# Block-sparse attention and a low-rank mixer: pair 5's turn, the first loads and the first scores rearranged

## The chip, the cores and the metric

The kernel runs on one core of one Trainium2 chip. The metric is the device time of one execution in microseconds (us), as the median of several runs. The engines are TensorE (PE, with its weight loads PEld), VectorE (DVE), ScalarE (ACT), GpSimd (POOL) and SyncE (SP, which here only issues transfers). PSUM is the memory that PE writes its products to, in 8 banks; SBUF is the working memory.

## The reference

Block-sparse attention over 4 batches, 8 heads, 768 positions and 64 channels, then a mixer over the result:

```python
scores = (q @ k.T) / sqrt(64)
# a 32x32 block is kept if it is on or next to the diagonal, in the first or last
# block row or column, or sampled; others get -1e9
attn = softmax(scores); x = attn @ v            # [4, 768, 512] with the heads side by side
h = x.transpose(0, 2, 1) @ U @ V                # U: 768x32, V: 32x768, over positions
u = x + h.transpose(0, 2, 1)
out = u + relu(u @ w_ch1) @ w_ch2               # 512 -> 2048 -> 512
```

Inputs and output are float32; the kernel computes its products in float16 with sums in float32.

## The kernel before, in words

Two heads make a **pair** (128 channels); there are 16 pairs, numbers 0 to 3 for batch 0, 4 to 7 for batch 1, and so on. The work of PE, DVE, ACT and SP is put in order by hand: `PLAN` is a long string of words, and each word issues one step. A capital letter is a step of PE, with the PSUM bank as its digit; a small letter takes what an earlier step left for ACT or DVE. Each engine works through its own instructions in the order in which the words name them and waits at semaphores.

- `S` and `B` are scores of batch 0 for one or two chunks of 128 keys (L697, L716). `e` is the exponential on ACT (L706, L724, and L750 for later batches).
- `A` multiplies exponentials with values for batch 0 (L400), `V` does so for later batches. `v` divides by the row sums on DVE (L472 to L477).
- `Q` and `H` are scores of batches 1 to 3 (L741), two heads side by side or one alone. `p` multiplies the exponentials with the mask on DVE (L756).
- `R` turns a loaded pair on PE (six 128x128 transposes against the identity `id16`, L670); `t` copies the result out of PSUM on DVE (L686 for batch 0, L684 for plain pairs). `Z` and `z` do the same for the second head of pair 0 (L337, L344).
- `K` and `k` make the 0/1 mask for the later batches (L656, L662). `M`, `m`, `X`, `Y`, `y`, `D`, `d`, `E`, `g` are the low-rank mixer.
- `U`, `P`, `C` are the first layer (L587), `a` and `b` its relu on ACT or DVE (L599, L601); `W`, `L` are the second layer (L611, L636), `f`, `l` the last sum and the store.

For batch 0 the mask is added inside the score product: `qres` holds the query's 64 channels and 24 one-hot rows, `kres` the key's 64 channels and 24 rows of biases. There are two such sets, `qres[0]`, `kres[0]` and `qres[1]`, `kres[1]`. The biases are computed at the very start from the sampled blocks (DVE, L289 to L296), multiplied with the one-hot rows on PE (`mask_half`, L271) and copied to `kres[0]` by `mask_row` (L279). The first products of `mask_half` lie in bank 6 and in bank 2. The second set's bias rows are copied by DMA (`second_set`).

**The head.** `first_load` fetches queries and keys of pair 0, one head at a time. `first_cast` makes them float16 (L210), `first_turn` turns them on PE in halves of 384 positions (L224), `first_row` copies them out (L282). Eight large dummy matmuls (`keep_warm`, L264) stand ahead of that, two small ones in the middle.

**Loads.** `load_qk(i)` and `load_v(i)` issue the loads of pair i on SP and its casts to float16 on POOL (L137 for whole tiles, L140 for pieces). `loads(i)` issues the loads of pair i+2; each kind has two load buffers. `front(i)` turns a pair by two DMA transposes on SP (L373). Pairs 1 to 4 are turned on PE by `R`, pairs 5 to 15 by `front`. POOL also issues the loads of the weights w1 (`load_w1`, behind the cast of pair 3's keys) and w2 (`hold`, L778 and L357: four one-element copies that wait for pair 5's keys as turned by `front(5)`, then four loads of 512 KB). `begin(i)` runs at the first score of pair i and issues loads at pairs 0, 1, 3 and 4.

Of the kernel before, what the change touches and what calls it, by code (L numbers as in the profile page):

```python
# [19 lines left out]
P = 128  # L20
# [3 lines left out]
def kernel(  # L24
# [43 lines left out]
    small_np = np.zeros((P, NB + 1 + P // 2), np.float32)  # L68
    small_np[:NB, :NB] = (ms_np - 1.0) * -MASK_BIAS
    small_np[:NB, NB] = ii  # L70
    small_np[:, NB + 1 :] = np.eye(P, dtype=np.float16).view(np.float32)

    small_dr = nc.inline_tensor(small_np, name="small_const")
    ohT_dr = nc.inline_tensor(ohT_np, name="one_hot_const")
# [36 lines left out]
    small = consts.tile([P, NB + 1 + P // 2], FP32)  # L111
    ms = small[0:NB, 0:NB]
    iota = small[0:NB, NB : NB + 1]
    id16 = small[:, NB + 1 :].bitcast(FP16)
# [54 lines left out]
    def first_load(h, n, queue):  # L169

        src, nm = ((q, "qld"), (k, "kld"))[n]
        if h == 0:
            lds[nm] = ldpool.tile([P, 2, T, D], FP32, tag="ld" + nm, name=nm)
            sts[0, nm] = stpool.tile([P, T, 2, D], FP16, tag="st" + nm, name="st" + nm)
        if h == 1:
            nc.gpsimd.memset(lds[nm][0:1, h, 0, 0:1], 0.0)
        queue.dma_start(
            out=lds[nm][:, h], in_=src[0, h].rearrange("(p t) d -> p t d", t=T)
        )

# [10 lines left out]
    def second_set():  # L191
        for h in range(2):
            one_hot(1, h)
# [14 lines left out]
    def first_cast(h, n, copy):  # L208
        nm = ("qld", "kld")[n]
        copy(out=sts[0, nm][:, :, h], in_=lds[nm][:, h])  # L210
# [3 lines left out]
    def first_turn(n, c):  # L214

        if n == 1:
            pt = psm([P, HS], FP32)
        elif c == 0:
            pt = pw[:, 1, 0:HS]
        else:  # L220
            pt = psc2()[:, 0, 0:HS]
        first_out[n, c] = pt
        for j in range(3):
            nc.tensor.matmul(  # L224
                pt[0:D, j * P : (j + 1) * P],
                sts[0, ("qld", "kld")[n]][:, 3 * c + j, 0],
                id16,
                start=(j == 0), stop=(j == 2), skip_group_check=True,
            )

    with tc.manual_schedule(
# [13 lines left out]
        first_load(0, 0, nc.sync)  # L245
        nc.scalar.dma_start(out=small, in_=small_dr.ap())
        first_load(0, 1, nc.scalar)
        for h in (1, 0):
            nc.vector.memset(qres[0][(slice(D, P), slice(0, D))[h], h, :], 0.0)
            one_hot(0, h)  # L250
        nc.vector.memset(bias, 0.0)
# [26 lines left out]
        def mask_row(h, c, copy):  # L278
            copy(out=kres[0][mrows[h], h, c * HS : (c + 1) * HS], in_=pks[c][mrows[h]])  # L279

        def first_row(n, c, copy):
            copy(  # L282
                out=(qres, kres)[n][0][drows[0], 0, c * HS : (c + 1) * HS],
                in_=first_out[n, c][0:D],
            )

        neq = consts.tile([P, NB, 3], FP32)
# [14 lines left out]
        for n in range(2):  # L302
            first_cast(0, n, nc.vector.tensor_copy)
        for c in range(2):
            first_turn(0, c)
            first_row(0, c, nc.scalar.copy)
        mask_half(0)
        mask_row(0, 0, nc.vector.tensor_copy)
        first_turn(1, 0)
        first_row(1, 0, nc.scalar.copy)  # L310
        first_turn(1, 1)
        mask_half(1)
        keep_warm(2, 256)
        first_row(1, 1, nc.vector.tensor_copy)
        mask_row(0, 1, nc.vector.tensor_copy)
        mask_row(1, 0, nc.vector.tensor_copy)
        mask_row(1, 1, nc.vector.tensor_copy)
# [3 lines left out]
        nc.vector.memset(Ut, 0.0)  # L321
        load_v(0)
        load_qk(1)
        second_set()
        load_v(1)
        load_mix()


# [105 lines left out]
    S0 S3 e e S5 B0 e Z7 e S3 z Z6 e z B0 A7 A e R6 S3 t A R5 e A B0 t A K6 e A S3 k v A5 A e K6  # L434
    k B0 A A e K7 A K6 k S3 k A K7 e v B0 k S3 e M6 e A5 A m R7 A t B0 K6 R3 e k A A t S6 A e v
    S0 D2 S3 e d A7 A e A S0 K6 A e S3 k K2 A e S5 k A e v S3 R2 e S5 t S0 e M7 e S3 m D2 e B5 d
    A0 D1 e A A d A S3 D2 A e d K1 S5 k R7 e S3 t A S1 e v A5 A e A S3 S6 e K2 A e A k A S3 v B0
    e K7 M6 e k S3 m X5 K7 e A6 Y k A B0 y X7 Y e S3 y E5 A e A g A R7 S0 t A e v S4 S2 e A7 A e
    R1 E6 A t A g A A Q v e e M6 X7 m Y P6 y p H U7 e p H b C e p H b U7 e p H b U6 e p E1 a g p
    V7 Q v e e V6 U7 v p U0 a P1 b C p P6 a C E7 Q a g U6 e e U7 b P6 b p U0 C a U7 p a Q b X6 Y  # L440
    e e P7 y C P6 b C p U0 b a p V7 Q v e e V6 W7 v p U0 W a p Q U6 e e W b U6 p W b p Q f W6 e
    e W p U2 U0 a p a V7 Q v W e e p V7 U2 v W a p Q f W7 e e W p U6 W a p Q U6 e e W b U6 p f a
    p V0 U1 v a V7 U6 v Q a M6 e e W7 m W p D6 U0 d U1 p a D2 D3 a U6 d d D0 U5 a d D6 U1 a d W
    a W Q f D6 W7 e e d W p D0 D6 W d d p W Q f W6 e e W p W W p Q f e e V7 U6 v p a V0 U2 v p
    U7 a U6 a Q b U7 e e U6 b U7 b p U2 a U6 p a U7 a Q b U6 e e U7 b U6 b p U2 a p a V7 Q v e e
    V6 U7 v p U0 b U1 a W6 p a Q W e e W p W U7 f p Q a U6 e e W7 b W p U1 p a V6 Q v W e e p V6
    U2 v W a p Q f W6 e e W p U7 W b p Q U7 e e W b U7 p f U2 a p a V0 v V7 W6 v Q M7 e e W m U7
    p D0 U1 a d U2 p a D7 D3 a U0 d d U1 a D5 D0 a U2 d d U7 a W a W Q f D7 W6 e e d W p D1 D7 W
# [452 lines left out]
```

## Time and profile before

| | us |
|---|---|
| median of 7 runs (lowest, highest) | 284.62 (283.57, 287.79) |
| the profiled execution | 283.55 |
| its span, from first to last instruction | 281.7 |
| first score on PE | 6.74 |
| first exponential on ACT | 7.27 |
| first exponential of pair 1 on ACT | 16.81 |
| first score of batch 1 on PE | 43.64 |
| first product of the first layer | 45.64 |
| busy time of PE, DVE, ACT, POOL | 273.7, 194.0, 177.9, 75.5 |

The span is the profiled one; the profiled execution is 1.85 us longer than its span, and 1.07 us shorter than the median. Matmuls on PE overlap one another, so the duration of one (218 ns for a 128-column transpose) is longer than the distance between the starts of two (about 55 ns), and the latter is what a further one costs. In the lines of the timeline the first number is the start in us, the second the busy time, then engine, line, operation, output<-input, shapes and count; square brackets hold the idle time before and what ended it.

### The profile page before, as it was taken

Reading aid. Unit: us, or ns where it says so; the run is one execution under the profiler, and the core shown is the slowest. Engines: PE = TensorE matmul, PEld = TensorE weight load, DVE = VectorE, ACT = ScalarE, POOL = GpSimd, SP = SyncE. Lnnn points to the kernel's source line nnn. Section 1 sums busy time; section 2 is a strip of 40 time slices with the busy share of each in tenths; the row PEclk is TensorE's granted clock in tenths of the full one; section 3 lists DMA queues with packets and bytes.
Section 4 is the critical chain, followed back from the end, with each engine's and each line's share of the span. In section 5 each row is a group of like instructions: output and inputs, shape, how many; then the busy total and the mean of one; then the engine's idle time right before and its main releaser. Section 6 shows DMA issues by size and latency. Waiting matters only on the chain.

```text
span 281.7 us, 6704 instructions
## 1 busy us (share of the span) xinstructions
PE 273.7 (97%) x2768; PEld 159.8 (57%) x2768; DVE 194.0 (69%) x347; ACT 177.9 (63%) x206; POOL 75.5 (27%) x164
## 2 busy tenths in 40 slices
PE   7899999999999999999999999999999999999993
PEld 3577775656464654656455654656547645555552
DVE  5689988988776898778677888776677871003411
ACT  3989998888668656686867555797776303451100
POOL 5369115901577050074352050060000000000000
PEclk9999999999999999999999999999999999999999
DMA  5789997999865654646350843740001062002021
GB/s 166 233 281 298 200 247 184 184 119 268 191 167 204 179 167 105 168 126 195 85 181 37 250 107 95 200 115 9 37 37 40 15 135 77 0 0 77 0 93 57
DMA packets 49118, 37.53 MB, mean 133 GB/s; under 512 B 30464, under 2 KB 45600, under 8 KB 49088
## 3 DMA queue, kind: packets, MB, share of 16 engines
q1 hardware_dynamic: 45968, 32.61, 41.7%
q0 software_dynamic: 2688, 4.19, 10.4%
q8 instruction: 21, 0.34, 0.5%
q10 hardware_dynamic: 432, 0.31, 0.4%
q14 instruction: 9, 0.07, 0.1%
HBM read 27.67 MB, written 6.29 MB: 121 GB/s over the span
## 4 chain that ended last, share of the span: by engine, by line
PE 90%; DMA 3%; DVE 2%; POOL 1%; ACT 1%; SPq 1%; issue 0%; DVEq 0%; ACTq 0%; POOLq 0%
PE ps L587 30%; PE ps L611 29%; PE ps L400 12%; PE ps L741 10%; DMA kld<-in_k_dram 2%; PE ps L697 2%; PE ps L529 2%; PE ps L716 2%; ACT est L724 1%; DMA out_dram<-of 1%; PE ps L670 1%; PE ps L636 1%; PE ps L656 1%; PE ps L566 0%; PE ps L498 0%; DVE xh L477 0%
## 5 line engine op out<-in xcount | busy, mean ns | idle before, releaser
L750 ACT ACTIVATE est<-ps 128x1536 f16<-128x1536 f32 x72 | 100.3, 1449 | 38.7 <-PE ps L741 38.7
L587 PE MATMUL ps<-uT,w1t 128*128 128x384 f16 x512 | 94.3, 326 | 0.0
L611 PE MATMUL ps<-w2t,tT 128*128 128x512 f16 x368 | 87.1, 379 | 0.0
L756 DVE TENSOR_TENSOR est<-est,mask 128x1536 f16<-128x1536 f16 x72 | 69.4, 969 | 15.0 <-ACT est L750 14.9
L599 ACT ACTIVATE tT<-ps 128x384 f16<-128x384 f32 x90 | 43.0, 494 | 43.5 <-PE ps L587 42.3
L587 PEld LDWEIGHTS <-w1t 128*128 128x128 f16 x512 | 47.6, 98 | 36.4 <-issue 5.8
L611 PEld LDWEIGHTS <-tT 128*128 128x128 f16 x368 | 34.5, 98 | 39.6 <-issue 3.8
L400 PEld LDWEIGHTS <-est 128*128 128x128 f16 x1152 | 40.8, 97 | 6.9 <-issue 1.9
L400 PE MATMUL ps<-vt,est 128*128 128x65 f16 x1152 | 43.4, 193 | 0.0
L140 POOL CAST stqld<-qld 128x192 f16<-128x192 f32 x40 | 18.8, 512 | 83.2 <-DMA qld<-in_q_dram 58.4
L619 DVE TENSOR_TENSOR of<-xf,ps 128x512 f32<-128x512 f32 x23 | 15.7, 684 | 27.7 <-PE ps L611 25.7
L601 DVE TENSOR_SCALAR tT<-ps 128x384 f16<-128x384 f32 x38 | 21.1, 555 | 19.0 <-PE ps L587 18.3
L741 PE MATMUL ps<-qpl,kpl 64*128 64x512 f16 (+1 forms) x288 | 31.3, 325 | 0.0
L706 ACT ACTIVATE est<-ps 128x768 f16<-128x768 f32 x30 | 22.5, 813 | 0.6 <-PE ps L697 0.6
L741 PEld LDWEIGHTS <-kpl 64*128 64x128 f16 x288 | 11.7, 94 | 15.9 <-issue 10.4
L477 DVE TENSOR_TENSOR xh<-ps,rcp 128x384 f16<-128x384 f32 x32 | 17.8, 558 | 1.1
L477 DVE TENSOR_TENSOR xf<-ps,rcp 128x384 f32<-128x384 f32 x32 | 17.5, 548 | 0.0
L140 POOL CAST stkld<-kld 128x192 f16<-128x192 f32 x40 | 16.7, 456 | 3.0 <-DMA kld<-in_k_dram 2.6
L541 DVE TENSOR_TENSOR xh<-xh,ps 128x384 f16<-128x384 f16 x28 | 15.4, 549 | 1.7 <-PE ps L529 1.6
L140 POOL CAST vt<-vld 128x192 f16<-128x192 f32 x40 | 15.8, 434 | 0.2 <-DMA vld<-in_v_dram 0.2
L542 DVE TENSOR_TENSOR xf<-xf,ps 128x384 f32<-128x384 f32 x28 | 15.3, 547 | 0.0
L697 PE MATMUL ps<-qres,kres 128*128 128x384 f16 x60 | 14.0, 324 | 0.8 <-DVE kres L279 0.5
(83 smaller groups left out, 149.4 us busy)
## 6 DMA issues: line engine op xcount, KB each, us to landing
vld<-in_v_dram SPq DMA_DIRECT2D x16, 384.0 KB, 5.3
out_dram<-of SPq DMA_DIRECT2D x23, 256.0 KB, 2.1
qld<-in_q_dram SPq DMA_DIRECT2D x15, 384.0 KB, 6.4
kld<-in_k_dram SPq DMA_DIRECT2D x15, 384.0 KB, 4.6
w1t<-in_moe_w_ch_dram POOLq DMA_DIRECT2D x4, 512.0 KB, 8.5
w2t<-in_moe_w_ch_dram POOLq DMA_DIRECT2D x4, 512.0 KB, 9.8
qld<-in_q_dram SPq DMA_DIRECT2D x2, 192.0 KB
uT<-xh SPq DMA_TRANSPOSE x14, 2.8
```

What stands on the lines that cost most here:

```text
L140: last = nc.gpsimd.tensor_copy(out=dst[:, h, ts], in_=ld[:, h, ts])
L400: nc.tensor.matmul(pav[:, sc, :], est[:, n, sc * P : (sc + 1) * P], vts[b % 2][:, 2 * hp + h, g, 0 : D + 1], start=(g == 0 and sc == 0), s ...
L477: nc.vector.tensor_tensor(out=dst, in0=pav[:, :, 0:D], in1=rcp[:, :, None].broadcast_to([P, T, D]), op=ALU.mult,)
L587: nc.tensor.matmul(pt, w1t[:, cc, jj * P : (jj + 1) * P], bts[b].uT[cc][:, c * HS : (c + 1) * HS], start=(cc == 0), stop=(cc == NCC - 1), ...
L599: nc.scalar.activation(out=dst, in_=pt, func=AF.Relu)
L601: nc.vector.tensor_scalar_max(out=dst, in0=pt, scalar1=0.0)
L611: nc.tensor.matmul(po, tts[b, c, jj][:, s * P : (s + 1) * P], w2t[:, jj, :], start=(jj == 0), stop=(jj == NJJ - 1),)
L697: nc.tensor.matmul(ps[:, c], kT[:, h, g * P : (g + 1) * P], qT[:, h, c * HS : (c + 1) * HS], start=True, stop=True,)
L706: lambda: nc.scalar.activation(out=dst, in_=ps, func=AF.Exp, scale=0.125),
L741: nc.tensor.matmul(units[h][:, u * S + lo : u * S + hi], kT[drows[h], g * P : (g + 1) * P], qT[drows[h], lo:hi], start=True, stop=True, sk ...
L750: nc.scalar.activation(out=both[h], in_=units[h].rearrange("p (g n) -> p g n", g=2), func=AF.Exp, scale=0.125,)
L756: lambda: nc.vector.tensor_mul(out=both[h], in0=both[h], in1=mask[:, 2 * j : 2 * j + 2, :]),
```

## The change

1. **First loads.** The queries of pair 0's first head go first on ACT's DMA queue. The small constants move to SP and lose the identity, which becomes a transfer of its own (`eye_dr`, 32 KB) on ACT's queue. The keys of that head come in two halves of 384 positions on SP, the second half behind the one-hot rows.
2. **First casts and turns.** ACT casts the queries and the first key half; DVE casts the second half later. The turns become PE transposes with float16 results. Of the first key half only the first 128 columns (keys and mask rows) are copied ahead of the first score, the rest behind. The two small dummy matmuls go. The second key half (`second_keys`: turn, copy, both copies of the second head's mask rows, and the zeros in `Ut`) comes behind the second score, with `second_set`, `load_v(1)`, `load_mix` and `loads(0)`.
3. **Pair 5** is turned on PE (two more `R` steps and two more `t` copies), not by DMA. The loads of pair 6 are issued behind the copy of pair 5's turned keys. `hold` goes: w2 is loaded behind the cast of pair 5's keys.
4. **PLAN** is another order of the same steps, with 10 `B` and 28 `S` for 9 and 30, and with 83 `a` and 45 `b` for 90 and 38.

```diff
-    id16 = small[:, NB + 1 :].bitcast(FP16)
+    id16 = consts.tile([P, P], FP16)
...
+    halves = (slice(0, T // 2), slice(T // 2, T))
...
-            nc.tensor.matmul(
-                pt[0:D, j * P : (j + 1) * P],
-                sts[0, ("qld", "kld")[n]][:, 3 * c + j, 0],
-                id16,
-                start=(j == 0), stop=(j == 2), skip_group_check=True,
+            nc.tensor.transpose(
+                out=pt[0:D, j * P : (j + 1) * P],
+                in_=sts[0, ("qld", "kld")[n]][:, 3 * c + j, 0],
+                identity=id16,
             )
...
-        first_load(0, 0, nc.sync)
-        nc.scalar.dma_start(out=small, in_=small_dr.ap())
-        first_load(0, 1, nc.scalar)
+        first_load(0, 0, nc.scalar)
+        nc.sync.dma_start(out=small[0:NB], in_=small_dr.ap())
+        first_load(0, 1, nc.sync, halves[0])
+        nc.scalar.dma_start(out=id16, in_=eye_dr.ap())
         for h in (1, 0):
             nc.vector.memset(qres[0][(slice(D, P), slice(0, D))[h], h, :], 0.0)
             one_hot(0, h)
+        first_load(0, 1, nc.sync, halves[1])
...
+        first_cast(0, 0, nc.scalar.copy)
...
         keep_warm(8)
-        for n in range(2):
-            first_cast(0, n, nc.vector.tensor_copy)
+        first_cast(0, 1, nc.scalar.copy, halves[0])
         for c in range(2):
             first_turn(0, c)
-            first_row(0, c, nc.scalar.copy)
-        mask_half(0)
-        mask_row(0, 0, nc.vector.tensor_copy)
         first_turn(1, 0)
-        first_row(1, 0, nc.scalar.copy)
-        first_turn(1, 1)
-        mask_half(1)
-        keep_warm(2, 256)
-        first_row(1, 1, nc.vector.tensor_copy)
+        for c in range(2):
+            mask_half(c)
+        first_row(0, 0, nc.scalar.copy)
+        first_row(0, 1, nc.vector.tensor_copy)
+        mask_row(0, 0, nc.vector.tensor_copy, 0, P)
+        first_row(1, 0, nc.scalar.copy, 0, P)
+        first_row(1, 0, nc.vector.tensor_copy, P)
+        mask_row(0, 0, nc.vector.tensor_copy, P)
+        first_cast(0, 1, nc.vector.tensor_copy, halves[1])
         mask_row(0, 1, nc.vector.tensor_copy)
-        mask_row(1, 0, nc.vector.tensor_copy)
-        mask_row(1, 1, nc.vector.tensor_copy)
...
-        nc.vector.memset(Ut, 0.0)
         load_v(0)
         load_qk(1)
-        second_set()
-        load_v(1)
-        load_mix()
-
+        for h in range(2):
+            one_hot(1, h)
+
+
+    def second_keys():
+        first_turn(1, 1)
+        first_row(1, 1, nc.vector.tensor_copy)
+        for c in range(2):
+            mask_row(1, c, nc.vector.tensor_copy)
+        nc.vector.memset(Ut, 0.0)
...
-    S0 S3 e e S5 B0 e Z7 e S3 z Z6 e z B0 A7 A e R6 S3 t A R5 e A B0 t A K6 e A S3 k v A5 A e K6
+    S0 S3 e e S5 B0 e Z7 e z Z6 S3 z e A7 B0 A A e R6 S3 t A A e A B0 v R6 e S4 t K3 K7 e k k B0
...
-                return nc.vector.tensor_copy(out=dst, in_=pt)
+                nc.vector.tensor_copy(out=dst, in_=pt)
+                if i == HP + 1 and n == 1:
+                    loads(HP)
+                return
...
+            elif i == 3:
+                with tc.issue_after(last.ins):
+                    load_w2(range(0, NJJ, 4))
-
-    def hold(behind):
-
-        for j in range(0, NJJ, 4):
-            nc.gpsimd.tensor_copy(out=w2t[0:1, j, 0:1], in_=behind[0:1, 0:1])
-        load_w2(range(0, NJJ, 4))
...
-        if i == HP:
-            front(HP + 1)
-        elif i == HP + 2:
+        if i == HP + 2:
...
-        for m in {0: (0,), 1: (1, 2), 3: (3,), 4: (4,)}.get(i, ()):
+        for m in {1: (1, 2), 3: (3,)}.get(i, ()):
             loads(m)
-        if i == HP:
-            hold(kpl[1])
...
-        "R": ((turn_qk, i, n) for i, n in each(range(1, HP + 1), (0, 1))),
+        "R": ((turn_qk, i, n) for i, n in each(range(1, HP + 2), (0, 1))),
...
-        for word in PLAN.split():
+        for x, word in enumerate(PLAN.split()):
+            if x == 2:
+                second_keys()
+                second_set()
+                load_v(1)
+                load_mix()
+                loads(0)
```

Around pair 5's two turns the new order reads `S1 g A Y e R6 y A A t A Q v R6 e e t M7 X6 m Y p E7 H`; the old one, without them, `S4 S2 e A7 A e R1 E6 A t A g A A Q v e e M6 X7 m Y P6 y p H` (`R1` there is pair 4's key turn).

## The prediction

> **What bounds the kernel now.** I read the page first (shares of the engines), then the stretches of time, then the timeline of the first 17 us, then the chain of waits around the end of the first batch, then the groups of VectorE (DVE) there.
>
> ```profile
> PE 273.7 (97%) x2768; PEld 159.8 (57%) x2768; DVE 194.0 (69%) x347; ACT 177.9 (63%) x206; POOL 75.5 (27%) x164
> ```
>
> TensorE (PE) is busy for 97% of the span. Where the other 3% lie, the stretches tell (span, busy time of PE, weight loads, DVE, ScalarE, GpSimd, granted clock, DMA share, GB/s):
>
> ```profile
> 6.74:12.00 5.26, 4.02 (x43) 2.64 (x42) 3.35 (x7) 4.47 (x6) 2.25 (x4) 1.00 0.69 229
> 12.00:16.00 4.00, 3.78 (x64) 2.87 (x60) 3.29 (x7) 3.49 (x4) 1.95 (x3) 1.00 0.78 202
> 16.00:46.00 30.00, 29.42 (x422) 21.58 (x421) 26.64 (x61) 27.73 (x33) 13.51 (x17) 1.00 1.01 246
> 46.00:270.00 224.00, 224.00 (x2169) 126.54 (x2169) 155.25 (x259) 139.52 (x161) 54.55 (x128) 1.00 0.48 117
> ```
>
> From 46 us on PE has no gap at all, at full clock. So nothing that the change does to transfers, GpSimd or relus after 46 us can gain time there; it can only lose some. PE's idle time after its first score (6.74 us) is 1.24 + 0.22 + 0.58 = 2.04 us, all before 46 us, and there ScalarE (27.73 of 30) and DVE (26.64 of 30) are nearly full as well. What can be gained is the 6.74 us ahead of the first score and these 2.04 us.
>
> ```profile
> 4.65 0.36 DVE L210 CAST stqld<-qld 128x384 f16<-128x384 f32 x1 [1.12 <-DMA qld<-in_q_dram]
> 5.07 0.52 PE L224 MATMUL ps<-small,stqld 128*64 128x128 f16 x6 [0.71 <-DVE stqld L210]
> 6.74 0.99 PE L697 MATMUL ps<-qres,kres 128*128 128x384 f16 x5
> 7.06 1.60 DVE L279 CAST kres<-ps 24x384 f16<-24x384 f32 x3
> 7.27 2.22 ACT L706 ACTIVATE est<-ps 128x768 f16<-128x768 f32 x3 [0.59 <-PE ps L697]
> 8.24 0.32 PE L697 MATMUL ps<-qres,kres 128*128 128x384 f16 x1 [0.52 <-DVE kres L279]
> 11.09 0.83 POOL L137 CAST stqld<-qld 128x768 f16<-128x768 f32 x1 [1.76 <-DMA qld<-in_q_dram]
> 11.97 0.51 PE L670 MATMUL ps<-small,stqld 128*128 128x128 f16 x6
> 16.81 1.45 ACT L724 ACTIVATE est<-ps 128x1536 f16<-128x1536 f32 x1 [0.20 <-PE ps L716]
> ```
>
> The reader is to see three gates in a row: the first query load (cast at 4.65), the third score, which waits for DVE's mask rows to leave PSUM bank 6 (8.24), and pair 1's query turn, which follows GpSimd's cast, which follows a load (11.92). The last line is pair 1's first exponential.
>
> **Part 1, the head.** Queries go first on ScalarE's queue: issued at 0.75 instead of 1.25. The constants, issued at 0.75, landed in 1.9 us with 44.5 KB; the 192 KB of keys took 3.7 us beside the queries. So the queries land between 2.65 and 4.1; I take 3.2, nearer the lone one. ScalarE's table load and first activation end at 3.15, its cast (0.36 as DVE's to 0.50 as GpSimd's) by 3.7. The key half lands between 3.6 and 4.6 (issued third on SP, at 1.65); its cast takes 0.2 to 0.3. The eight warming matmuls stand from 0.79 to 4.36 with the last one's drain, so PE is free at 4.2 and turns from 4.2 to 5.1 wherever the loads land in those ranges. Nine 128-column turns at 0.055 us between starts and two mask products follow: 4.2 + 0.5 + 0.33 = 5.03. Copies: the first rows left PSUM 0.39 us after the turn's start (5.07 to 5.46) and took 0.47; then a third of the key columns (0.2), beside a third of the mask columns. First score 4.2 + 0.39 + 0.47 + 0.2 + 0.1 = 5.4, at the late end 6.3. **That is 1.3 us earlier (0.4 to 1.4).** The two 256-column warming matmuls that go (0.24 us) stood in PE's wait for the copies and save nothing.
>
> What is late next: the third score writes bank 6, from which DVE still copies the second head's mask rows. DVE's queue from 4.8: query half 0.3, mask 0.2, keys 0.25, mask 0.4, key cast 0.2, mask 0.53, key half 0.3, mask 0.53 (16-bit copies by the 768 columns in 0.56 of L344, 32-bit ones by 1.60/3), with waits for PE 0.3: 7.8 against 8.24. Lead 0.45.
>
> Then pair 1. Its loads stand on SP behind the same things as before; the later ones wait for GpSimd's memset at 3.23 in both. The cast that ends at 11.92 stays, so the turn at 11.97 stays: lead 0 at this point. The new order puts the next double score ahead of the key turn, and the score after it needs the keys' first copy only: by DVE, query copies 12.55 to 13.65, division 14.85 (rows of 1.1 and 1.2), key copy 15.4. Pair 1 starts at 15.5 against 15.96: lead 0.46. Seven mask copies (0.55 each) stand ahead of pair 1's second head on DVE; the second use of bank 6 waits for them until about 19.05, and PE then has 1.6 us of work up to the double score that began at 20.72: 20.6. **Lead 0.15 from here on**; bounds 0 and 1.3.
>
> **Part 2, pair 5's turns.** Two steps R more, 12 matmuls. Two DMA transposes go from SP; the four small copies ahead of the W2 loads on GpSimd go.
>
> ```profile
> 40.27 0.34 PE ps L670 x6
> 43.97 0.57 DVE xh L477
> 44.59 0.51 PE ps L498 x6
> 45.12 0.30 DVE a L502
> 45.47 0.34 PE ps L513
> ```
>
> The row: six turns cost 0.34 us of PE, so +0.67. The query turn stands where PE waits for the last exponential of the batch: hidden, or 0.34 where that wait is gone. The key turn falls between the double score (43.64 + 0.76 = 44.40) and L498 at 44.59, so 0.19 of its 0.34 is hidden. But both copies go to DVE:
>
> ```profile
> L684 DVE COPY qpl<-ps 128x768 f16<-128x768 f16 x1 | 0.6, 559 | 0.3 <-PE ps L670 0.3
> L684 DVE COPY kpl<-ps 128x768 f16<-128x768 f16 x1 | 0.6, 558 | 0.4 <-PE ps L670 0.4
> ```
>
> 0.56 us each. The key copy stands ahead of the copy of `a` (45.12), for which PE's L513 waits: the division ends at 45.0, key copy 45.56, `a` 45.85, L513 at 45.9 instead of 45.47. L529 (0.17) now comes behind that, so the next score starts at 46.23 instead of 46.06, and 0.16 more of PE work is left behind it (0.33 of a first-layer step moved back, 0.17 moved ahead). **Sum +0.33, plus 0.07 for the query turn: +0.4**; bounds +0.15 and 0.67 + 1.12 = +1.8 (nothing hidden on PE or DVE).
>
> The Trainium skill ("TensorE: Matmul & The Clock Gate", Part 4: PE-mode transpose) speaks against this part: a 128x128 turn there is about 275 ns in a kernel, the clock does not come up for it, and a copy has to follow. By that page, as an estimate, the twelve would cost 3.3 us and the total would be near 287.5. The rows of this case show 218 ns from start to end, pipelined to 55 ns between starts, at a granted clock of 1.00; I go by them.
>
> **Part 3, transfers.** Pair 5's loads stand on SP right behind pair 0's `uT` transpose, which moves from 29.9 us to about 24; before, they were issued at 35.31, behind both. Its casts wait for pair 3's turns (27.0 and 32.0 before), so they end near 33 instead of 43. W2 is then issued near 33 instead of 48.38, and its first product stands at 68.5. Its 2 MB and pair 5's 1.15 MB share the DMA engines with w1, whose four loads landed by 38.6 (the landings in the trace); 1.15 MB at the 298 GB/s of the page's fullest slice is 3.9 us: 42.5, and the first product with w1 stands at 45.6. Cover 3.1 us; beyond it each us costs one. Pair 6's loads come behind pair 5's key copy, at 45.6 against 45.54. Cost 0.
>
> Seven relus pass from ScalarE (0.49) to DVE (0.55); 46 to 270 us shows DVE at 155 of 224, cost 0, and 0.4 if all seven land on full stretches. One double score replaces two single ones on ScalarE: 1.35 against 2 x 0.71, 0.07 less.
>
> **Sum.** The profiled execution took 283.55 us, a span of 281.70 and 1.85 around it. 283.55 - 0.15 + 0.4 = 283.8. The median of seven runs lies 1.07 above that execution, so 284.9. A measurement of this kernel tells a change from none at about 1%, 2.85 us.
>
> **Rivals.** *The lead lasts.* If pair 1's queries land early (GpSimd waited 1.76 us for them) nothing holds the order up: -1.3 + 0.4 = -0.9, 284.0; with PE's 2.04 us of waits gone as well -2.9, 281.7, just over 1%. For it: PE, ScalarE and DVE all follow the first score. Against: 11.92 is set by a load whose place does not change, and DVE has little room.
>
> *DVE becomes the bound, slower.* Place: 16 to 46 us, DVE 26.64 of 30. The two copies (1.12) and PE's 0.67 land in full and the lead is eaten: +1.8, 286.4. It decides once DVE's idle time there, 3.4 us now, falls under some 1.1 us. Against: most of that idle time must go first.
>
> *Pair 6 or w1 late, slower.* Pair 6's first score stands at 66.5; before, its transposes were issued by 57.3 and landed 2.8 us later. Cover some 6 to 9 us, against W2's 2 MB in the way. If it were 4 us late beyond that: 288.9.
>
> *The change does not do what it says*, W2 staying behind the w1 loads in GpSimd's queue: no time, as above.
>
> **How the numbers follow.** No change as computed 0.60; the lead lasts 0.23, a quarter of that beyond 1%; DVE 0.11; late transfers 0.06. Faster by over 1% 0.07, slower by over 1% 0.08 (late transfers, and 0.02 of DVE's case), within 1% 0.85. The likeliest case alone spans 283.8 to 286.0 (its lead 0 to 1.3, its cost 0.15 to 0.8, and half a us of scatter in the median); the range takes in most of the first two rivals: 282.6 to 287.0.
>
> **What would show it.** Right: first score near 5.4, first exponential near 5.9; third score waiting for DVE's L279-like copies near 7.8; pair 1's query turn still near 12; first score of batch 1 (L741-like) within 0.5 us of 43.64; no PE gap after 46. Wrong: a first score of batch 1 before 42.5 or after 45, or PE waiting for `w1t`, `w2t` or pair 6's rows.

## The result, and the profile after

| | before | after |
|---|---|---|
| median, us (lowest, highest) | 284.56 (283.04, 288.75), 59 runs | 285.71 (284.38, 287.82), 24 runs |
| ratio to before, 95% interval | | 1.0047 (1.0026 to 1.0068) |
| span of the profiled execution | 281.70 | 284.01 |

The change makes the kernel slower by 0.3 to 0.7%, which lies inside the 1% called no change. The forecast of 284.9 us (282.6 to 287.0) holds the 285.71. Its sum was +0.25 us; the medians differ by 1.15, the ratio says about +1.3, the two profiled executions +2.3. Runs of one and the same kernel fall into groups 1 to 3 us apart, so medians settle little under half a per cent here; below, the starts of certain matmuls (landmarks) in the traces carry the argument, and the distances between them repeat to some hundredths in kernels that share a part.

PE's line of the page after, against the first line shown of before:

```profile
PE 276.1 (97%) x2778; PEld 160.9 (57%) x2778; DVE 199.4 (70%) x358; ACT 176.0 (62%) x199; POOL 78.1 (27%) x160
```

The stretches after, cut as those of before (span, busy time of PE, weight loads, DVE, ACT, POOL, granted clock, DMA share, GB/s):

```profile
6.09:12.00 5.91, 4.98 (x28) 2.79 (x29) 4.01 (x10) 3.77 (x4) 3.42 (x5) 0.71 0.72 225
12.00:16.00 4.00, 4.00 (x62) 3.04 (x61) 2.24 (x6) 3.43 (x4) 1.94 (x3) 1.00 0.85 270
16.00:46.00 30.00, 28.42 (x427) 21.19 (x427) 26.60 (x60) 27.44 (x31) 13.94 (x19) 1.00 1.05 262
46.00:270.00 224.00, 223.61 (x2175) 125.83 (x2172) 160.75 (x271) 138.32 (x155) 55.92 (x123) 1.00 0.44 111
```

Two things are new. Up to 12 us the granted clock is 0.71, and PE, busy for 4.00 of 4.00 us right behind it, does work that has become late. And from 16 to 46 us PE idles 1.58 us instead of 0.58, with DVE and ACT no busier than before. After 46 us little changes.

The gates of the head, in the timeline after (start, busy time, engine, line, operation, what it waited for):

```profile
6.09 0.48 PE L708 MATMUL ps<-qres,kres 128*128 128x384 f16 x2 [0.31 <-DVE kres L280]
7.11 0.56 DVE L280 CAST kres<-ps 24x384 f16<-24x384 f32 x1
...
7.97 1.00 DVE L280 CAST kres<-ps 24x384 f16<-24x384 f32 x2
8.56 0.48 PE L708 MATMUL ps<-qres,kres 128*128 128x384 f16 x1 [0.76 <-DVE kres L280]
...
9.95 0.83 POOL L137 CAST stqld<-qld 128x768 f16<-128x768 f32 x1 [0.41 <-DMA qld<-in_q_dram]
...
13.35 0.49 PE L678 MATMUL ps<-id,stqld 128*128 128x128 f16 x6
...
17.88 1.45 ACT L735 ACTIVATE est<-ps 128x1536 f16<-128x1536 f32 x1 [0.20 <-PE ps L727]
```

The first score comes 0.65 us earlier than before (6.74), but the third one comes 0.32 later (8.24 before), pair 1's query turn 1.38 later (11.97), and pair 1's first exponential 1.07 later (16.81). GpSimd's cast, which was to hold pair 1's turn, ends at 10.78 and holds nothing.

What PE waits for between 12 and 56 us (engine, line, waited for, total us, times, longest). The kernel before has no entry in this view; after has six, five of them for DVE:

```profile
PE ps L727 <- DVE xf L550: 0.4, 1, 0.4
PE ps L727 <- DVE a L510: 0.3, 1, 0.3
PE ps L727 <- ACT est L735: 0.3, 1, 0.3
PE ps L506 <- DVE xf L485: 0.2, 1, 0.2
PE ps L664 <- DVE mask L670: 0.2, 1, 0.2
PE ps L708 <- DVE xf L550: 0.2, 1, 0.2
```

L727 (`B`), L708 (`S`) and L664 (`K`) write scores and masks of batch 0 into PSUM banks that DVE is still reading: `xf` is the last reader of a mixer product (L550) or of a value product (L485), `a` the copy of the mix. For instance, the mix M5 (L506) goes into bank 5 and, one score later, the double score B5 (L727) into banks 5 to 7, so it waits for the copy `a`. In the old PLAN the words at that place are M7, S3, m, D2, B5, with one step of PE more between copy and score.

The turn to batch 1, on PE, before and after:

```profile
43.64 0.82 PE L741 MATMUL ps<-qpl,kpl 64*128 64x512 f16 x8
...
46.06 0.82 PE L741 MATMUL ps<-qpl,kpl 64*128 64x512 f16 x4
46.81 0.82 PE L587 MATMUL ps<-uT,w1t 128*128 128x384 f16 x4
47.57 0.82 PE L741 MATMUL ps<-qpl,kpl 64*128 64x512 f16 x4
...
51.84 1.26 PE L400 MATMUL ps<-vt,est 128*128 128x65 f16 x36
53.03 0.82 PE L741 MATMUL ps<-qpl,kpl 64*128 64x512 f16 x8
```

```profile
45.74 0.82 PE L752 MATMUL ps<-qpl,kpl 64*128 64x512 f16 x8
...
48.55 1.69 PE L752 MATMUL ps<-qpl,kpl 64*128 64x512 f16 x8
50.17 1.15 PE L595 MATMUL ps<-uT,w1t 128*128 128x384 f16 x6
...
53.19 1.47 PE L595 MATMUL ps<-uT,w1t 128*128 128x384 f16 x8
54.50 1.26 PE L408 MATMUL ps<-vt,est 128*128 128x65 f16 x36
55.69 0.82 PE L752 MATMUL ps<-qpl,kpl 64*128 64x512 f16 x8
```

From the first score of batch 1's first pair to that of its second it takes 9.39 us before and 9.95 after. The old order puts first-layer steps between the single scores; the new one puts two of them back to back (48.55) and eight first-layer matmuls in one block ahead of the value products (53.19). Both orders have 16 first-layer matmuls in this stretch; the new one has the six of pair 5's key turn besides.

### The profile page after: what moved, and what is told of

Same layout as the page of the kernel before. It is cut to its first block, busy times and chain, and to the rows that moved or that the text cites. A ratio compares the mean times of both kernels' runs of the same rounds, so it can differ in the third digit from the quotient of the medians.

```text
span 284.0 us, 6722 instructions
## 1 busy us (share of the span) xinstructions
PE 276.1 (97%) x2778; PEld 160.9 (57%) x2778; DVE 199.4 (70%) x358; ACT 176.0 (62%) x199; POOL 78.1 (27%) x160
## 4 chain that ended last, share of the span: by engine, by line
PE 84%; DVE 2%; DMA 1%; issue 1%; ACT 1%; ACTq 0%; DVEq 0%
PE ps L595 30%; PE ps L619 28%; PE ps L408 10%; PE ps L752 10%; PE ps L537 2%; PE ps L727 1%; DMA out_dram<-of 1%; PE ps L644 1%; PE ps L708 1%; ACT est L761 1%; PE ps L574 0%; DVE kres L697 0%; DVE xf L550 0%; DVE qres L697 0%; PE ps L678 0%
## 5 line engine op out<-in xcount | busy, mean ns | idle before, releaser
L761 ACT ACTIVATE est<-ps 128x1536 f16<-128x1536 f32 x72 | 100.4, 1448 | 38.1 <-PE ps L752 38.0
L607 ACT ACTIVATE tT<-ps 128x384 f16<-128x384 f32 x83 | 39.9, 494 | 46.6 <-PE ps L595 45.6
L140 POOL CAST stqld<-qld 128x192 f16<-128x192 f32 x40 | 17.2, 474 | 88.5 <-DMA qld<-in_q_dram 59.6
L609 DVE TENSOR_SCALAR tT<-ps 128x384 f16<-128x384 f32 x45 | 25.0, 556 | 20.9 <-PE ps L595 19.9
L717 ACT ACTIVATE est<-ps 128x768 f16<-128x768 f32 x28 | 21.3, 809 | 2.5 <-PE ps L708 2.3
L140 POOL CAST stkld<-kld 128x192 f16<-128x192 f32 x40 | 19.3, 521 | 0.2 <-POOL stqld L140 0.2
L140 POOL CAST vt<-vld 128x192 f16<-128x192 f32 x40 | 18.9, 511 | 0.0
L485 DVE TENSOR_TENSOR xh<-ps,rcp 128x384 f16<-128x384 f32 x32 | 17.8, 557 | 1.1
L485 DVE TENSOR_TENSOR xf<-ps,rcp 128x384 f32<-128x384 f32 x32 | 17.5, 548 | 0.0
L735 ACT ACTIVATE est<-ps 128x1536 f16<-128x1536 f32 x10 | 14.5, 1452 | 2.6 <-PE ps L727 2.6
L708 PE MATMUL ps<-qres,kres 128*128 128x384 f16 x56 | 14.2, 333 | 1.4 <-DVE kres L280 1.2
```

The lines of the kernel that those rows point to most:

```text
L140: last = nc.gpsimd.tensor_copy(out=dst[:, h, ts], in_=ld[:, h, ts])
L485: nc.vector.tensor_tensor(out=dst, in0=pav[:, :, 0:D], in1=rcp[:, :, None].broadcast_to([P, T, D]), op=ALU.mult,)
L607: nc.scalar.activation(out=dst, in_=pt, func=AF.Relu)
L609: nc.vector.tensor_scalar_max(out=dst, in0=pt, scalar1=0.0)
L708: nc.tensor.matmul(ps[:, c], kT[:, h, g * P : (g + 1) * P], qT[:, h, c * HS : (c + 1) * HS], start=True, stop=True,)
L717: lambda: nc.scalar.activation(out=dst, in_=ps, func=AF.Exp, scale=0.125),
```

## The experiments

e1 to e4, e5 to e8 and e9 to e12 ran on three chips, on which the kernel before had medians of 284.71, 283.71 and 283.60; so medians of different groups are compared by their ratios to it.

One table for all: starts of matmuls in the trace of each kernel. "S" is the first score, "Q" the first score of batch 1 (pair 4), "Q2" the first score of pair 5, "last" the last product, "end" the end of the span. "Rise" is when the profile first has the granted clock at 1.00. Ahead of it the profile has no clock record, and a view prints 1.00 there too; the first turns after, which ran ahead of the rise, stand 0.107 us apart instead of 0.055.

| kernel | S | S to Q | Q to Q2 | Q2 to last | last to end | rise |
|---|---|---|---|---|---|---|
| before | 6.74 | 36.90 | 9.39 | 224.00 | 4.67 | 4.47 |
| e4 new head alone | 5.78 | 37.56 | 9.40 | 223.99 | 4.05 | 3.40 |
| e8 e4 and dummies | 6.36 | 37.56 | 9.40 | 223.99 | 4.06 | 5.98 |
| e5 e8 and new order | 5.76 | 38.42 | 9.96 | 223.96 | 4.06 | 4.25 |
| e1 e5 and pair 5 on PE | 5.65 | 38.43 | 10.03 | 224.14 | 4.18 | 4.10 |
| after | 6.09 | 39.65 | 9.95 | 224.16 | 4.16 | 5.11, half from 8.52 to 11.94 |
| e2 after, pair 5 by DMA | 6.16 | 39.62 | 9.96 | 224.06 | 4.06 | 5.25, half from 8.66 to 12.08 |
| e6 order alone, old head | 7.88 | 39.16 | 9.96 | 223.95 | 4.66 | 12.26 |
| e3 order and pair 5, old head | 8.13 | 38.31 | 9.96 | 223.95 | 4.75 | 10.01 |
| e12 after, two dummies | 5.61 | 38.42 | 9.96 | 223.95 | 4.17 | 3.88 |

Here "order" is the new PLAN with w2's new place. Columns that agree among kernels with the same part, and differ from all others, say what the part is worth: Q to Q2 is 9.4 with the old order and 9.95 to 10.03 with the new one, whatever the head.

**e1: the clock held up.** The changed kernel with dummy matmuls in PE's waits: two ahead of the first score, eight between the turn of the second key half and the third score.

```diff
+        keep_warm(2, 256)
         first_row(0, 0, nc.scalar.copy)
...
     def second_keys():
         first_turn(1, 1)
+        for _ in range(8):
+            nc.tensor.matmul(
+                bank(5, [P, 256], FP32), warm[:, 0:P], warm[:, 0:256], start=True, stop=True
+            )
```

> The changed kernel with ten dummy matmuls of 256 columns more, all in TensorE's waits: two ahead of the first score, eight between the turn of the second key half and the third score. Theory (clock): in the profile of the changed kernel the granted clock of 5 to 12 us is 0.76, because TensorE did too little between 5.1 and 8.5 us; at half speed it fell 1.9 us behind by the first score of pair 0's second head. With the dummies the clock stays at 1.00 from 5 to 12, pair 1's first exponential (17.88) comes 1 to 1.5 us earlier, and the median falls from 285.7 to 284.4 to 284.8. Rival (order and pair 5): ScalarE and VectorE bound that stretch anyway, the clock comes up but the first score of batch 1 stays within 0.4 us of 45.74 and the median within 0.4 of 285.7.

Measured: 285.19 (283.91 to 286.56), ratio 1.0008 (0.9975 to 1.0041); span 282.43. The stretches of 3.41 us in which the clock is set, after and then in e1:

```profile
1.70:5.11 3.41, 3.41 (x15) 1.45 (x14) 1.58 (x7) 2.56 (x5) 1.66 (x6) 1.00 0.67 187
5.11:8.52 3.41, 2.21 (x14) 0.74 (x12) 3.08 (x9) 1.99 (x4) 0.96 (x2) 1.00 0.97 313
8.52:11.94 3.42, 3.38 (x19) 2.27 (x19) 1.63 (x4) 2.26 (x2) 2.46 (x3) 0.50 0.58 175
```

```profile
4.10:7.51 3.41, 3.23 (x26) 1.62 (x26) 2.66 (x8) 2.28 (x5) 0.95 (x2) 1.00 0.95 274
7.51:10.93 3.42, 3.18 (x34) 2.21 (x32) 2.44 (x6) 2.62 (x4) 1.46 (x2) 1.00 0.74 256
```

(The first row lies ahead of the rise at 5.11.) In the profiled execution after, PE is busy for 2.21 of 3.41 us, and in the next stretch the clock is 0.50: the first double score takes 1.48 us there (at 8.84), against 0.81 in e1 (at 8.28). With the dummies the clock stays at 1.00 and S to Q falls by 1.22 us (39.65 to 38.43). So the theory holds in the trace; the median lies between what the two expected. By the ratios e1 lies 0.4% below after, but the two intervals overlap. The mean granted clock of each run points the same way: it is 0.994 or 0.995 in 5 of 24 runs of after and 0.991 to 0.994 in 5 of 12 of e2, and never under 0.996 in the 12 of e1. The other 19 runs of after have 0.997 or more, so the fall of the clock is a matter of some executions, the profiled one among them.

**e2: pair 5 back on DMA transposes**, its four words out of PLAN, all else as after.

```diff
-    ... A Y e R6 y A A t A Q v R6 e e t M7 X6 ...
+    ... A Y e y A A A Q v e e M7 X6 ...
...
+        if i == HP:
+            front(HP + 1)
-        if i == HP + 2:
+        elif i == HP + 2:
```

> The changed kernel with pair 5 turned by two DMA transposes at the first score of batch 1, as before, and pair 6 loaded there; the four words of pair 5's turns leave the order, all else stays. Clock theory with the prediction's price for the turns: 0.4 to 0.7 us less, 285.0 to 285.3, and the clock of 5 to 12 us still falls in some executions. Rival (pair 5 is the whole loss): 1.1 us less or more, 284.6 or below.

Measured: 285.04 (283.90 to 286.45), ratio 1.0007 (0.9978 to 1.0036); span 283.86. The median is in the range that the theory gave; its interval overlaps with after's, and the landmarks are the same (39.62, 9.96). The clock fell in this profile as well. Pair 5 is not the whole loss.

**e3 and e4: the two halves of the change.** e3 is before with all that is new but the head; e4 is before with the new head alone.

```diff
-        first_load(0, 0, nc.sync)
-        nc.scalar.dma_start(out=small, in_=small_dr.ap())
-        first_load(0, 1, nc.scalar)
+        first_load(0, 0, nc.scalar)
+        nc.sync.dma_start(out=small[0:NB], in_=small_dr.ap())
+        first_load(0, 1, nc.sync, halves[0])
...
```

That diff with the rest of the head's is e4. e3 has the other lines:

```diff
-    S0 S3 e e S5 B0 e Z7 e S3 z Z6 e z B0 A7 A e R6 ...
+    S0 S3 e e S5 B0 e Z7 e z Z6 S3 z e A7 B0 A A e R6 ...
...
-        "R": ((turn_qk, i, n) for i, n in each(range(1, HP + 1), (0, 1))),
+        "R": ((turn_qk, i, n) for i, n in each(range(1, HP + 2), (0, 1))),
```

> The kernel before with everything new but the head: the new order of steps, pair 5 on TensorE, the new places of pair 6's and w2's loads; the first loads, casts, turns and copies stay as they were. Clock theory: the clock stays at 1.00 in 5 to 12 us as before, and what is left is pair 5's price, 284.56 + 0.4 to 0.8 = 285.0 to 285.4. Rival (the head costs nothing, order and pair 5 cost all): 285.7, or more, since the head's lead is missing.

> The kernel before with the new head alone; order of steps, pair 5, pair 6 and w2 as before. Clock theory: the clock falls below 1.00 in 5 to 12 us in many executions and costs up to 1.9 us there, less the 0.65 us that the first score gains: 284.6 to 285.6. Rival (the head's lead lasts, the clock does not matter): 283.6 to 284.2, faster than before.

Measured: e3 286.65 (285.30 to 288.50), ratio 1.0079 (1.0043 to 1.0114); e4 283.75 (282.59 to 285.80), ratio 0.9964 (0.9928 to 1.0000). Both go against the clock theory and with the rivals: the rest of the change is a loss of more than was forecast, and the head is a gain, though its interval touches 1.0000. The clock rose only at 10.01 in e3's profile, and fell in few of e4's runs (a mean of 0.992 in 2 of 12). The table shows where e4 gains: its first score is 0.96 earlier, S to Q gives back 0.66, and the end of the program, from the last product on, is 0.62 shorter.

**e5: the order with the clock held.** The edits of e1 and e2 together: the new head, the new order, the dummies, pair 5 by DMA.

> The changed kernel with the ten dummy matmuls of e1 and with pair 5's queries and keys back on DMA transposes, its four words out of PLAN: what is left of the change is the head, the order and W2's place, at a clock that the dummies hold up. Theory (pair 5's turns on TensorE cost 0.5 to 1.1 us, more than the 0.4 forecast, and the order costs the rest): 284.4 us median, 0.5 to 1.1 less than e1's 285.19, ratio to before 0.996 to 1.001, and the profiled span 281.5 to 282.0. Rival (pair 5 costs only its PE time beyond the waits it fills, 0.2 or less, and the order alone is the price): 285.0 or more, level with e1, span 282.3.

Measured: 284.07 (283.87 to 284.65), ratio 1.0001 (0.9982 to 1.0019); span 282.16. The median lies 1.1 us below e1's, as the theory had it, but e1 ran where the kernel before was itself 1.00 slower; the ratios, 1.0001 and 1.0008, don't tell the two apart, and the span is nearer to the rival's. The trace decides: against e1, S to Q differs by 0.01, Q to Q2 by 0.07, the rest by 0.18. Pair 5's turns on PE cost 0.26 us there, and nothing in e12, which has them too and shows e5's numbers (38.42, 9.96, 223.95). So they cost 0 to 0.26, and the theory's 0.5 to 1.1 falls. They stand in waits that the new order has without them (from Q to Q2 PE idles 0.96 us in e5 and 0.41 in e1); what they would cost in the old order, no run here shows.

**e6: the order alone**, which is e3 with e2's edit: the old head, the new order, pair 5 by DMA.

> The kernel before with its own head, pair 5 on DMA transposes as before, and of the change only the new PLAN (less the four words of pair 5) and W2's place. Theory (the new order costs 0.8 to 1.3 us in batch 0, most of it where the division of pair 0's first head stands ahead of the copy of pair 1's turned keys): 285.6 us median, ratio 1.003 to 1.006, the first score of batch 1 at 44.4 to 45.0 us in the profile where before has 43.64. Rival (the order is neutral, as the prediction had it, and e3's loss is the old head together with pair 5): 284.7, ratio 1.000, first score of batch 1 at 43.6 to 43.9.

Measured: 285.96 (284.90 to 287.75), ratio 1.0067 (1.0037 to 1.0097). The order costs, and the rival that called it neutral is out. Its size can't be read from this profile's first score of batch 1 (47.04), since here the clock rose only at 12.26. With the clock held it is read from e5 against e8: S to Q +0.86, Q to Q2 +0.56, the rest -0.03, so 1.4 us. The two stretches of e5, then of e8:

```profile
5.76:44.18 38.42, 36.24 (x512) 26.46 (x512) 32.31 (x72) 34.43 (x38) 17.28 (x24) 1.00 1.01 244
44.18:54.14 9.96, 9.00 (x92) 4.88 (x90) 9.07 (x15) 8.76 (x7) 3.52 (x5) 1.00 0.93 152
```

```profile
6.36:43.92 37.56, 36.25 (x513) 26.77 (x511) 32.41 (x72) 34.29 (x39) 17.84 (x24) 1.00 0.98 250
43.92:53.32 9.40, 9.19 (x92) 4.78 (x91) 8.77 (x16) 8.54 (x7) 6.11 (x15) 1.00 0.93 211
```

PE does the same work in both orders; what grows is its idle time, 2.18 us against 1.31 up to Q and 0.96 against 0.21 from there to Q2. So the order costs by waits.

**e7: the division behind the key copy.** One word of e1's PLAN moved.

```diff
-    ... A A e A B0 v R6 e S4 t K3 K7 e k k B0
+    ... A A e A B0 R6 e S4 t v K3 K7 e k k B0
```

> e1 (the changed kernel and ten dummy matmuls) with one word of PLAN moved: the division of pair 0's first head (v) goes behind the copy of pair 1's turned keys (t) on VectorE's queue. Theory (that division makes pair 1's first scores wait and the wait is not won back): PE's wait ahead of pair 1's first value product goes, 0.4 to 0.8 us less than e1, 284.5 median, ratio to before 0.996 to 1.000, profiled span 281.6 to 282.0. Rival (VectorE is behind with its work as a whole there, so the wait only moves to the next copy): the same as e1, 285.2, span 282.2 to 282.6.

Measured: 285.85 (285.51 to 287.35), ratio 1.0076 (1.0050 to 1.0103), S to Q 39.64 instead of 38.43, at a clock of 1.00 from 5.94 on. It is slower by 1.2 us in the trace, against both expectations. PE's longest wait, and DVE's timeline there:

```profile
PE ps L669 <- DVE xf L490: 2.1, 1, 2.1
```

```profile
14.98 1.12 DVE L702 COPY kres<-ps 64x768 f16<-64x768 f16 x2 [0.86 <-POOL vt L137]
16.12 0.20 DVE L485 RECIPROCAL rcp<-ps 128x6 f32<-128x6 f32 x1
16.35 0.56 DVE L490 TENSOR_TENSOR xh<-ps,rcp 128x384 f16<-128x384 f32 x1
16.83 0.55 DVE L490 TENSOR_TENSOR xf<-ps,rcp 128x384 f32<-128x384 f32 x1
```

The mask product K7 (L669) writes bank 7, out of which the division reads. Put behind the key copy, the division ends at 17.4, and K7 waits for it. In this order the place of `v` is tied from both sides: ahead of `t` it delays pair 1's scores, behind it K7.

**e8: e4 with the dummies**, the same lines as in e1.

> e4 (the kernel before with the new head alone) and the ten dummy matmuls. Theory (the new head is worth about 0.9 us with the old order, and its clock falls only in a part of the executions): 283.3 to 283.8 us median, ratio 0.995 to 0.998, clock 1.00 from its first rise on in the profile, no execution at 0.99 clock. Rival (the dummies stand in the way of the real work, or the clock of e4 never fell): 283.7 to 284.2, no better than e4's 283.75.

Measured: 283.51 (282.68 to 285.02), ratio 0.9983 (0.9958 to 1.0009). No difference to e4 can be told from the ratios. S to Q is 37.56 in both: the clock did not fall in e4's profile either, and the dummies take nothing from the old order. No run is under 0.998 of the clock, where e4 had two at 0.992, as the theory had it.

**e9 and e10: `xf` off VectorE.** In batch 0 the second product of the division is replaced by a copy on GpSimd, in e1 (e9) and in e8 (e10).

```diff
-            for dst in (
-                self.xh[:, :, h * D : (h + 1) * D],
-                self.bt.xf[:, :, head * D : (head + 1) * D],
-            ):
+            xh = self.xh[:, :, h * D : (h + 1) * D]
+            xf = self.bt.xf[:, :, head * D : (head + 1) * D]
+            for dst in (xh,) if self.i < HP else (xh, xf):
                 nc.vector.tensor_tensor(
...
+            if self.i < HP:
+                nc.gpsimd.tensor_copy(out=xf, in_=xh)
```

> e1 (the changed kernel and ten dummy matmuls) with the division's second product, xf (0.55 us on VectorE out of PSUM, eight heads in batch 0), taken off VectorE: GpSimd copies it from xh instead. That frees a value product's PSUM bank 0.55 us earlier and every VectorE instruction queued behind the division. Theory (the new order costs because it takes banks and copies over sooner than VectorE, which divides first, lets go of them): most of TensorE's waits for VectorE in batch 0 go, 0.7 to 1.3 us less than e1's 285.19, 284.2 median, ratio to before 0.994 to 0.999, first score of batch 1 at 43.0 to 43.6 us after a first score near 5.7 (e1: 44.07). Rival (the waits are ScalarE's exponentials in another guise): level with e1, first score of batch 1 at 44.0. A mishap is possible: GpSimd's casts are late behind the copies, and it is slower than e1.

> The same as e9 on e8, which has the new head and the dummies but the old order and pair 5 on DMA transposes. It is the control for e9. Theory (the old order hardly waits for VectorE, whose waits in the trace of e8 come to 0.9 us, all before 13 us): 0 to 0.3 us less than e8's 283.51. Rival (a shorter VectorE queue helps any order): 0.7 or more less than e8, as in e9.

Measured: e9 294.36 (293.82 to 295.55), ratio 1.0347 (1.0302 to 1.0391); e10 291.03 (290.28 to 292.58), ratio 1.0231 (1.0186 to 1.0276). The mishap won. DVE's wait and PE's in e9, and GpSimd's timeline:

```profile
DVE xf L568 <- POOL xf L494: 8.6, 1, 8.6
PE ps L413 <- DVE xf L568: 8.1, 1, 8.1
```

```profile
28.54 0.98 POOL L494 CAST xf<-xh 128x384 f32<-128x384 f16 x2
40.93 0.83 POOL L137 CAST stqld<-qld 128x768 f16<-128x768 f32 x1 [11.41 <-DMA qld<-in_q_dram]
...
45.95 0.52 POOL L494 CAST xf<-xh 128x384 f32<-128x384 f16 x1
```

A copy of 0.5 us stands in GpSimd's queue behind a cast that waits 11.4 us for a load, and DVE's queue, and then PE, wait for that copy. The clock fell with it, to 0.50 from 43.42 to 53.66 us. In e10 PE has three waits for DVE of 1.2 to 1.9 us, two of them for `xf`, and the clock is 0.50 from 57.23 to 64.05. The experiment does not tell the theory from its rival, since the mishap covers both. GpSimd's 14 idle us of 30 (16 to 46 us in e1) were not free: they are waits in a queue that works in order.

**e11: two banks exchanged at the turn to batch 1**, in e5.

```diff
-    ... Q v e e M7 X6 m Y p E7 H y ...
+    ... Q v e e M6 X7 m Y p E7 H y ...
```

The step E7 then writes bank 7 ahead of the copy `y`, so the columns that `y` copies there are other numbers than the reference's; the instructions are the same.

> e5 (changed kernel, dummies, pair 5 on DMA) with the banks of two words exchanged: at the turn to batch 1 the mix of pair 4's channels goes into bank 6 and the turn back into bank 7 (M6 X7, as the kernel before has it) in place of M7 X6. In e5 that mix waited 0.59 us for the division's second product, which still read bank 7. Theory (that wait is the bank's alone): 0.4 to 0.6 us less than e5's 284.07, so 283.6, ratio to before 0.997 to 0.9995, and no wait for xf ahead of the mix. Rival (the mix needs xh of the same division anyway and the wait is given back at the next copy): 284.0, level with e5.

Measured: 284.22 (283.63 to 284.67), ratio 0.9989 (0.9961 to 1.0018). The mix no longer waits for `xf`, but PE now has this wait among the scores of the same stretch:

```profile
PE ps L754 <- ACT est L763: 0.5, 1, 0.5
```

Q to Q2 is 9.96 as in e5. The ratio lies in the range of the theory, but its interval holds e5's too, so the trace decides: the rival was right in what counts, the wait was given back, though at the exponentials and not at a copy. In this order, freeing that bank alone gains nothing.

**e12: the two small dummies put back** into the changed kernel, ahead of the first score.

```diff
+        keep_warm(2, 256)
         first_row(0, 0, nc.scalar.copy)
```

> The changed kernel with only the two dummy matmuls of 256 columns put back that the change took out (keep_warm(2, 256), here ahead of the first score). Theory (the clock falls because TensorE does too little between 6 and 8.5 us, and two dummies at 5.5 to 6 us are ahead of most of that stretch): the clock still falls in a part of the executions, 285.2 to 285.7 median, ratio 1.002 to 1.005. Rival (these two alone held the clock): as e1, 285.1 or less, ratio near 1.001, and no execution below 0.996 of the clock.

Measured: 285.36 (284.71 to 287.80), ratio 1.0051 (1.0015 to 1.0086). In its profile the clock held (rise at 3.88), by the ratio it is no better than after, and 2 of its 12 runs have a mean clock of 0.995. That is as the theory had it, though two runs are few. No version clearly beats both kernels: e4 at 0.9964 touches 1.0000 with its interval.

## Why the prediction was right, and where only its sum was

The forecast "no change" came true in part by luck: terms that it had too small or at nothing went both ways. It had -0.15 for the lead and +0.4 for pair 5. The runs have -0.33 (e8) to -0.92 (e4) for the head, by when the clock rises, +1.4 for the order and 0 to 0.26 for pair 5, so +0.5 to +1.3, and 1.2 more where the clock falls. Of the +2.31 us between the two profiled spans, by the table: first score -0.65, S to Q +2.75, Q to Q2 +0.56, the rest +0.16, the end -0.51. The 2.75 fall to the head (e4 against before, +0.66), the order (e5 against e8, +0.86), pair 5 (e1 against e5, +0.01) and the clock (after against e1, +1.22). Without the clock's 1.22 it is +1.09, which is about what the medians show; in most runs of after the clock did not fall.

- **First score: right within its bounds, for the lead.** 5.4 was forecast with 6.3 as the late end; it came at 5.6 to 5.8 in profiles whose clock rose by 4.3 us, and at 6.1 to 6.4 where it rose between 5.1 and 6.0. The step took the turns at 0.055 us each; in the profile after they ran before the rise, 0.107 apart.
- **Third score, 7.8: late with the first.** It came at 8.56, and instead of a lead of 0.45 it lost 0.32. The list of copies on DVE was right: 2.4 us from the first score to the third were forecast, and it was 2.47. But the queue began later: its first copy of the queries started at 5.18, not at 4.8, since it waited for PE. In e12, with its first score at 5.61, the third came at 8.08, a lead of 0.16.
- **Pair 1's turn held by GpSimd's cast at 11.92: wrong in the reason.** The cast ended at 10.78 after, so the load came earlier; e1 has the turn at 11.70, held by PE's own queue. After has it at 13.35, because of the clock. With the clock up, pair 1's first double score starts at 15.38 (e1) and 15.48 (e5), as forecast (15.5).
- **"Lead 0.15 from here on" is the step that failed.** At 20.5 us it was still true: e5 starts the sixth double score at 20.50, against 20.6 forecast and 20.72 before (before, then e5):

```profile
20.72 0.81 PE L716 MATMUL ps<-qres,kres 128*128 128x512 f16 x4
```

```profile
20.50 0.81 PE L729 MATMUL ps<-qres,kres 128*128 128x512 f16 x4
```

  But the working stopped there and took the remaining 24 us of batch 0 and the turn to batch 1 as they were before. From this score to Q e5 takes 23.68 us and before 22.92, and from Q to Q2 it takes 0.57 more: that is where most of the new order's waits lie, four of the six lines above among them. The term was 0 and measured 1.3, of the order's 1.4 in all.
- **Pair 5's turns, +0.4 (0.15 to 1.8): right in mechanism.** 0 to 0.26 by e1, e12 and e5. All of it is hidden or nearly so. By the figure in the Trainium skill ("TensorE: Matmul & The Clock Gate", Part 4: PE-mode transpose) the estimate was 3.3 us; the runs say otherwise.
- **Transfers, 0: right in the cost, not in the times.** W2's loads were forecast near 33 us and were issued at 44.60, since pair 5's casts began at 41.05; W2's first product stands at 73.1. There is no wait of PE for `w1t`, `w2t` or pair 6's rows after 46 us; Q2 to the last product is 224.0 to 224.2 in both.
- **"The two warming matmuls save nothing", and a clock of 1.00 throughout: wrong.** The clock was taken over from the profile before as if it were a property of the kernel. Its fall cost 1.2 us in the profile after and in e2's, and shows in 5 of 24 and 5 of 12 of their runs.
- **The end of the program** is no term of the sum; it gave 0.5 back.
- **Slips that change nothing here:** 284.62 - 0.9 is 283.7, not 284.0; the likeliest case begins at 283.0 by its own terms, not at 283.8; with 3.3 in place of 0.4 the total is 287.8, not 287.5.

*The lead lasts* did not come true: e4, where the lead was alone, has Q 0.30 us earlier, not 1.3. *DVE becomes the bound* came nearest: it gave the sign. But DVE is as busy as before from 16 to 46 us (26.60 against 26.64) and its idle time never fell to the point that was named. PE's waits name the moment at which a bank is let go, not the amount of DVE's work; e9 and e10, which were to test this, leave it open.

## What to carry to other kernels

When an order is rewritten by hand, walk each bank from its last reader to its next writer over the whole stretch that changed; an engine with 3 us to spare still makes another wait if the reader stands one step ahead of the next writer. An idle engine whose queue works in order is not free: look at what stands in the queue ahead of the new instruction. And a head that leaves PE waiting in small pauses can lose the clock with it; read the granted clock by its own stretches before saying that fewer matmuls cost nothing.

## What the runs showed of the hardware that was not expected

- **The clock moves in steps of 3.41 us whose phase differs from execution to execution**: first rises at 3.40 to 6.03 us in the eleven profiles with the new head, the later changes whole multiples of 3.41 behind. With the old head and the new order it rose at 10.01 (e3) and 12.26 (e6). There PE stands idle for 0.96 and 0.71 us behind the eight dummies, and in the new head it does not; that the late rises come from this is not shown, since before has the same pause and rose at 4.47.
- **It fell although PE was busy for 2.21 of 3.41 us and its longest pause was 0.76 us** (after); in e2 the stretch from 5.25 to 8.66 had 2.17. In before a stretch with 2.33 kept the clock:

```profile
4.47:7.88 3.41, 2.66 (x21) 1.52 (x22) 2.53 (x6) 1.83 (x4) 1.00 (x2) 1.00 0.83 266
7.88:11.30 3.42, 2.33 (x22) 1.57 (x22) 2.27 (x5) 3.42 (x5) 1.04 (x2) 1.00 0.69 228
```

  The Trainium skill ("TensorE: Matmul & The Clock Gate", Part 1) has the free-running window of about 3.4 us, which these runs show, and says that the clock falls after an idle window; here a window that was busy for two thirds was enough. Part 4 of that page says that transposes don't count as busy in the same way. That alone does not explain it: without its transposes PE is busy for 1.82 us in the stretch of after and 1.85 in e2's, where the clock fell, and for 1.82 in the second row of before and 1.83 in e12 (7.29 to 10.70), where it stayed. Nor is it the busy time alone that lets the clock rise: in e6 the stretch from 5.44 to 8.85, two steps ahead of 12.26, had PE busy for 3.41 of 3.41 us, and the clock did not rise at its end. What counts stays open.
- **The end of the program is 0.6 us shorter with the new head**: 4.66 to 4.75 us from the last product's start in the three kernels with the old head, 4.05 to 4.18 in all others. The difference lies behind the issue of the last store, from which it takes 3.04 to 3.16 and 2.44 to 2.57 us to the end. The cause stays open.
